# A gated network kernel's start: batch 1's k turned on TensorE, weights in longer runs, first loads issued by ScalarE, a new order of steps

## The chip, the cores and the metric

The kernel runs on one core of a Trainium2 chip. Its time is the device time of one execution in microseconds (us), taken as the median of three runs. The profile shows one further execution, instruction by instruction; its span is the time from its first instruction to the end of its last one.

## What is computed

For each of 8 batches, linear attention over 8 heads (576 rows, 64 channels a head) makes x, and a gated network works on x:

```python
q_s = softmax(q, axis=-1);  k_s = softmax(k, axis=2)        # k over its 576 rows
x = einsum('bhsd,bhde->bhse', q_s, einsum('bhsd,bhse->bhde', k_s, v))   # -> (8, 576, 512)
h = gelu_tanh(x @ w_in)                                      # w_in 512 x 1024
u, v = h[..., :512], h[..., 512:]
v_n = (v - mean(v)) / sqrt(var(v) + 1e-6) * g_ln
v_s = einsum('ts,bsd->btd', w_sg, v_n) + b_sg[None, :, None] # w_sg 576 x 576
out = x + (u * v_s) @ w_out                                  # w_out 512 x 512
```

w_in and w_out are float64; all other inputs and the output are float32.

## The kernel before

**Steps and order.** The program is a list of named steps, `PLAN`; each names a small function with a batch and the piece it works on. A step issues a few instructions on one engine, and every engine runs its own in the order of the list (line 163 for the engines, line 253 for TensorE), so the list is the queue of each engine and of SP, which issues all transfers. An instruction that waits holds up everything behind it on its engine. At the end of a step's name, `V`, `A` and `G` choose VectorE, ScalarE or GpSimd for it.

**Precision.** Every float32 operand of the large products is split into a high part that TensorE takes in its fast format and a low part; a product is high x high, high x low and low x high in one accumulation. w_in and w_out are float64, so each arrives as two 32-bit words and is made into float32 on the chip, then split: `wi_a` (ScalarE scales), `wi_b`, `wi_c`, `wi_d` (VectorE shifts and merges), `wi_h` (ScalarE writes the high part) and `wi_l` (the low part), once for each of w_in's eight pieces of 128 columns (512 KB), with `wo_*` for w_out's four; `ws_h` and `ws_l` split w_sg's five pieces. Pieces 0 to 3 of w_in make u, 4 to 7 make v.

**A batch.** `load_q`, `load_k`, `load_v` bring the inputs, each batch in two halves of four heads (the second number of a step). q: maximum, subtraction, exponential, sum, inverse, product, then a transpose to `qt`. Batch 0's q lies flat and is worked in two groups a half (`qf_*`, the third number) and turned by TensorE (`qtr_mm`, `qf_copy`); the other batches' q is turned by VectorE (`q_turn`). k: batch 0 arrives with its rows along the free axis (`k_turn`), so a maximum over rows is one instruction (`kr_max`), ScalarE takes the exponential (`kr_exp`), TensorE turns it back with ten transposes a half (`ktr_mm`) and ScalarE copies it out (`kr_copy`, `kr_rest`). Batch 1's k arrives the other way round: VectorE folds the rows (`k_ma`, `k_mb`, `k_mc`), TensorE turns the 128 partial maxima (`kt_mm`), VectorE reduces (`k_top`), TensorE spreads the result (`kb_mm`), VectorE subtracts (`k_sub`) and ScalarE takes the exponential (`k_exp`). Batches 2 to 7 use a fold on VectorE instead of TensorE. `kv_mm` forms k's product with v, `kv_scale` divides, and `xf_mm` (batch 0, in four pieces), `x_mm` (batch 1) or `xm_mm` make x; `xf_high`, `xf_low` and their like write its two parts.

**The network.** `hu_mm` makes a piece of u (batch 0 in two column groups, `hu_part`, emptied by `hu_gpart` with the gelu), `hv_mm` a row block of v, `hv_gelu`, `hv_sq`, `hv_stat`, `hv_pow`, `hv_norm`, `hv_high`, `hv_low` its normalisation, `sg_mm` the product with w_sg, `gate`, `gate_high`, `gate_low` the gating, `out_mm` the last product, `out_base`, `out_add`, `out_store` the end. TensorE writes large groups into three double PSUM banks in turn and small ones into two single banks in turn (`bank`), so a group waits until the one three (or two) before it is emptied. `warm` multiplies the identity by itself and its result is not read.

**Names that are shared.** The tile `x_l` has two buffers: batch 0's turned k lies in the first until `ktr_mm` has read it. The tile of q of one half is shared by all batches, so `load_q 1 1` waits until batch 0's second half was turned. `load_v 2 1` waits for `kv_mm 1 1`, which reads the tile it writes.

## Time and profile before

| | us |
|---|---|
| median of three runs (lowest, highest) | 498.81 (498.34, 499.73) |
| the profiled execution, its own time | 498.2 |
| its span | 496.4 |
| TensorE busy with matmuls | 483.7 (97%) |
| VectorE, ScalarE, GpSimd busy | 357.8, 285.8, 180.0 |
| transfers | 47.08 MB on SP's queue |

The granted TensorE clock is 0.999 of full over the span. Busy times are unions of an engine's instructions; matmuls overlap one another, so a busy TensorE may still be waiting in part. Most instructions stand under line 164, the helper that issues them, and all matmuls under line 253; they are told apart by their tiles (`ps<-x_h,wi_h` is a matmul of x's high part with w_in's). `x_lk` is the turned k, `raw_i_*` are w_in's words, `kk` is k, `km` its maxima, `qq` is q.

### The profile page before, as it was taken

The page shows a single profiled execution, that of the slowest core. Times are in us where ns is not written, and L with a number is a line of the kernel's source. Part 1 is how long each engine was busy: PE and PEld are TensorE (multiplying, and loading weights), DVE is VectorE, ACT ScalarE, POOL GpSimd, SP SyncE. Part 2 cuts the span into 40 slices and gives each one's busy share as a digit, 9 for nine tenths or more (in the row PEclk, how much of TensorE's full clock was granted, in tenths as well). Part 3 has the DMA queues.
Part 4 walks back from the last instruction along what each step waited for, and adds up shares of the span by engine and source line. Part 5 has one row for each costly group of instructions (what it writes and reads, how often), then busy time and mean ns, then how long its engine had stood idle before and what let it go on. Part 6 is the DMA issues. An engine that isn't in the chain of part 4 may idle for free.

```text
span 496.4 us, 9521 instructions
## 1 busy us (share of the span) xinstructions
PE 483.7 (97%) x3859; PEld 445.4 (90%) x3859; DVE 357.8 (72%) x608; ACT 285.8 (58%) x603; POOL 180.0 (36%) x138
## 2 busy tenths in 40 slices
...
GB/s 278 362 380 208 153 172 1 157 105 136 1 58 242 53 45 49 76 56 120 97 57 141 93 61 47 1 71 167 39 2 1 144 73 1 1 0 49 1 1 143
DMA packets 20911, 47.68 MB, mean 96 GB/s; under 512 B 1922, under 2 KB 9476, under 8 KB 20868
## 3 DMA queue, kind: packets, MB, share of 16 engines
q1 hardware_dynamic: 20868, 47.08, 27.7%
...
## 4 chain that ended last, share of the span: by engine, by line
PE 68%; DVE 18%; DMA 4%; ACT 4%; issue 3%; POOL 2%; SPq 1%; DVEq 0%; ACTq 0%; POOLq 0%
PE ps L253 68%; DVE km L164 3%; DMA raw_i_vnl<-w_in 2%; DVE qm L164 2%; DVE v L164 1%; DVE ot_i L164 1%; DVE qd L164 1%; DMA x_lk<-k_turn 1%; DVE kf L164 1%; POOL qq L164 1%; DVE ot_o L164 1%; DMA vv<-v 1%; DVE o L164 1%; SPq L164 1%; DVE vnl L164 1%
## 5 line engine op out<-in xcount | busy, mean ns | idle before, releaser
L164 POOL TENSOR_TENSOR rs<-ve,half 128x1 f32<-128x1 f32 (+1 forms) x37 | 30.4, 826 | 98.6 <-DVE ve L164 98.6
L253 PE MATMUL ps<-ws_h,vnl 128*128 128x288 f32 x256 | 55.0, 296 | 0.7 <-DVE vnl L164 0.7
L253 PE MATMUL ps<-ulow,wo_h 128*128 128x288 f32 x256 | 55.6, 296 | 0.0
L253 PE MATMUL ps<-gh,wo_h 128*128 128x288 f32 x256 | 55.5, 295 | 0.0
L253 PE MATMUL ps<-gh,wo_l 128*128 128x288 f32 x256 | 55.3, 295 | 0.0
L253 PE MATMUL ps<-ws_h,vnh 128*128 128x288 f32 x256 | 55.2, 297 | 0.0
L253 PE MATMUL ps<-ws_l,vnh 128*128 128x288 f32 x256 | 54.9, 296 | 0.0
L164 POOL TENSOR_TENSOR ulow<-u,gh 128x576 fp32r<-128x576 f32 x17 | 28.0, 1644 | 67.3 <-ACT gh L164 56.6
L164 POOL TENSOR_TENSOR qq<-qq,qm 128x1152 f32<-128x1152 f32 (+2 forms) x13 | 26.5, 2039 | 63.5 <-DVE qm L164 43.8
L164 DVE TENSOR_TENSOR u<-ps,u 128x576 f32<-128x576 f32 x32 | 23.9, 749 | 32.3 <-PE ps L253 32.2
L164 ACT ACT_TABLE_LOAD x34 | 43.6, 1283 | 5.8 <-PE ps L253 2.7
L164 ACT CAST gh<-u 128x576 fp32r<-128x576 f32 x32 | 21.1, 668 | 42.8 <-DVE u L164 42.7
L253 PEld LDWEIGHTS ps<-ws_h,vnh 128*128 128x128 f32 x256 | 41.5, 188 | 0.8
L253 PEld LDWEIGHTS ps<-ws_h,vnl 128*128 128x128 f32 x256 | 41.1, 188 | 0.9 <-DVE vnl L164 0.9
L253 PEld LDWEIGHTS ps<-gh,wo_h 128*128 128x128 f32 x256 | 41.3, 188 | 0.6
L253 PE MATMUL ps<-x_h,wi_h 128*128 128x288 f32 (+2 forms) x256 | 40.7, 299 | 0.7 <-ACT x_l L164 0.7
L253 PEld LDWEIGHTS ps<-gh,wo_l 128*128 128x128 f32 x256 | 41.3, 188 | 0.0
L253 PEld LDWEIGHTS ps<-ulow,wo_h 128*128 128x128 f32 x256 | 41.1, 188 | 0.1
L253 PE MATMUL ps<-wi_h,x_h 128*128 128x512 f32 (+1 forms) x148 | 41.0, 398 | 0.0
L253 PEld LDWEIGHTS ps<-ws_l,vnh 128*128 128x128 f32 x256 | 41.0, 188 | 0.0
L253 PE MATMUL ps<-wi_h,x_l 128*128 128x512 f32 (+1 forms) x148 | 40.9, 396 | 0.1
L253 PE MATMUL ps<-wi_l,x_h 128*128 128x512 f32 (+1 forms) x148 | 40.5, 395 | 0.0
...
## 6 DMA issues: line engine op xcount, KB each, us to landing
...
```

The source lines that it names most:

```text
L164: ins = op(*args, **kw)
L253: tc.keep_in_program_order(nc.tensor.matmul(*args, **kw))
```

## The change

Four things are changed together. Batch 1's k arrives turned as batch 0's does and goes through `kr_max`, `kr_exp`, `ktr_mm`, `kr_copy` and `kr_rest`; it lies in the second `x_l` buffer. w_in and w_out are laid out in memory by pieces, so that a partition's part of one piece is one run of 4096 bytes instead of four of 1024. The identity, the two bias rows and the two turned loads of batch 0's second half are issued by ScalarE, ahead of everything else on it. And the order of the steps and the engine of many of them (`V`, `A`, `G`) are new from the first step to the last; seven warm steps stand where eight did, three of them ahead of the first turned q instead of seven in a row. In the diff, `PLAN` is cut after the first `sg_mm` of either version.

```diff
 FOLD = [2, 3, 4, 5, 6, 7]
 ALONE = [0, 1]
-TURN = [0]
+TURN = [0, 1]
 FLAT = [0]
-SHAPES = [(B - len(FLAT), 2, P, 2, 18, 32), (len(FLAT), 2, P, 18, D), (B - len(TURN), 2, P, 5, 256), (len(TURN), 2, P, 2, S), (B, 2, P, 5, 4, D + 1), (DM, 2048), (1, DV), (5, P, WT), (1, WT), (DV, 1024), (P, P), (B, DM, S)]
+SHAPES = [(B - len(FLAT), 2, P, 2, 18, 32), (len(FLAT), 2, P, 18, D), (B - len(TURN), 2, P, 5, 256), (len(TURN), 2, P, 2, S), (B, 2, P, 5, 4, D + 1), (8, P, 1024), (1, DV), (5, P, WT), (1, WT), (4, P, 1024), (P, P), (B, DM, S)]
 
...
 PLAN = """
-kr_zero 0 1, load_q 0 1 1, qf_max 0 1 1, qf_sub 0 1 1 V, qf_exp 0 1 1, load_q 0 1 0, kr_zero 0 0, qf_max 0 1 0, qf_sub 0 1 0 G, qf_exp 0 1 0, load_eye
-warm 0, warm 1, warm 9, warm 7, warm 4, load_q 0 0 0, qf_max 0 0 0, warm 8, warm 6, qf_sum 0 1 1, load_k 0 0 1, kr_max 0 0 1, kr_exp 0 0 1
-load_q 0 0 1, qf_sub 0 0 0 G, qf_exp 0 0 0, qf_inv 0 1 1, qf_mul 0 1 1 G, qf_max 0 0 1, qf_sub 0 0 1 G, load_k 0 0 0, kr_max 0 0 0, kr_exp 0 0 0
-load_k 0 1 0, kr_max 0 1 0, kr_exp 0 1 0, load_w_in 1, qf_exp 0 0 1, wi_a 1, qf_sum 0 0 0, qf_inv 0 0 0, load_w_in 0, ktr_mm 0 0, qf_sum 0 1 0
-kr_copy 0 0, qf_sum 0 0 1, qf_inv 0 0 1, wi_a 0, wi_b 1, kr_rest 0 0, neg, load_k 0 1 1, kr_max 0 1 1, qtr_mm 0 1 1, load_v 0 0, qf_mul 0 0 0 G
-qtr_mm 0 0 0, wi_b 0, qf_mul 0 0 1 G, warm 2, qf_copy 0 1 1, qf_inv 0 1 0, qf_mul 0 1 0 G, kr_exp 0 1 1, qf_copy 0 0 0, load_w_in 2, wi_a 2, kv_mm 0 0
-qtr_mm 0 0 1, wi_c 0, kv_inv 0 0, load_w_in 3, kv_scale 0 0, wi_c 1, wi_d 0, qf_copy 0 0 1, wi_a 3, load_v 0 1, ktr_mm 0 1, kr_copy 0 1, qtr_mm 0 1 0
-qf_copy 0 1 0, wi_b 2, xf_mm 0 0 0, kr_rest 0 1, kv_mm 0 1, wi_b 3, xf_high 0 0 0, wi_c 2, wi_h 0, wi_c 3, wi_d 1, wi_h 1, wi_d 3, wi_h 3, load_w_sg 1
-wi_l 0 V, xf_low 0 0 0, xf_mm 0 0 1, wi_x 3, xf_high 0 0 1, kv_inv 0 1, kv_scale 0 1, xf_mm 0 1 0, xf_mm 0 1 1, wi_d 2, load_w_in 7, wi_a 7, wi_b 7
-xf_high 0 1 0, xf_neg 0 0 1, load_k 1 0, wi_c 7, k_ma 1 0, xf_high 0 1 1, xf_neg 0 1 0, wi_d 7, k_mb 1 0, xf_low 0 1 1, xf_low 0 0 1 A, hu_part 0 0 1
-load_w_in 4, wi_l 1 G, xf_low 0 1 0 A, load_q 1 1, k_mc 1 0, kt_mm 1 0, load_k 1 1, wi_a 4, wi_b 4, wi_h 2, hu_part 0 0 0, wi_l 2 G, hu_gpart 0 0 1
-hu_part 0 2 0, load_w_in 5, q_max 1 1, k_ma 1 1, k_mb 1 1, wi_c 4, wi_d 4, wi_h 7, k_mc 1 1, q_swapm 1 1, q_top 1 1, q_sub 1 1 G, hu_gpart 0 0 0
-wi_a 5, wi_b 5, wi_l 3 A, load_q 1 0, q_max 1 0, wi_h 4, hu_part 0 1 0, hu_gpart 0 2 0, hu_gpart 0 1 0, load_w_in 6, wi_a 6, kt_mm 1 1, k_top 1 1
-ws_h 1, hu_part 0 3 0, hu_gpart 0 3 0, q_swapm 1 0, k_top 1 0, kb_mm 1 0, load_w_sg 2, wi_b 6, wi_l 7 V, q_exp 1 1, load_w_out 3, wi_c 5, wi_c 6
-load_w_out 0, load_g, q_top 1 0, load_b, q_sub 1 0 G, wi_d 6, wi_h 6, k_sub 1 0 V, k_exp 1 0, hu_part 0 2 1, wi_d 5, wi_l 6 G, load_v 1 0, q_exp 1 0
-hu_part 0 1 1, wi_h 5, b_h, kb_mm 1 1, k_sub 1 1 V, k_exp 1 1, q_sum 1 0, load_w_sg 0, hu_part 0 3 1, q_swapd 1 0, q_sum 1 1, wi_l 4 G, kv_mm 1 0
-kv_inv 1 0, kv_scale 1 0, q_inv 1 0, q_swapd 1 1, wi_l 5 G, b_l G, q_inv 1 1, hv_mm 0 0, hv_gelu 0 0 A, load_w_out 2, hu_gpart 0 3 1, q_mul 1 0 0 V
-q_mul 1 0 1 G, q_turn 1 1, q_mul 1 1 1 G, q_turn 1 0, hu_gpart 0 1 1, load_w_sg 3, hv_mm 0 3, hv_gelu 0 3 A, load_v 1 1, hu_gpart 0 2 1, ws_h 2
-q_turn 1 3, kv_mm 1 1, x_mm 1 0, kv_inv 1 1, kv_scale 1 1, q_mul 1 1 0 G, q_turn 1 2, wo_a 3, wo_z 3, x_high 1 0, x_low 1 0, wo_a 0, wo_b 0, wo_c 0
-hv_mm 0 1, ws_h 0, wo_b 3 A, wo_d 3, load_w_out 1, wo_a 1, wo_a 2, hv_sq 0 0, hv_stat 0 0 A, hv_norm 0 0, hv_gelu 0 1 A, hv_sq 0 1, wo_b 2, ws_l 0 V
-wo_d 0, x_high 1 1, load_q 2 1, hv_stat 0 1 A, hv_sq 0 3, wo_b 1, wo_c 1, wo_d 1, x_mm 1 1, x_high 1 3, hv_mm 0 4, hv_pow 0 0, x_high 1 2
-hv_stat 0 3 A, hv_norm 0 3, x_neg 1 1, hv_mm 0 2, hv_pow 0 3, x_low 1 1 A, hv_gelu 0 4 A, wo_c 2, wo_d 2, hv_pow 0 1, ws_l 2 G, x_low 1 2, x_low 1 3
-load_w_sg 4, hv_high 0 0, hv_low 0 0, ws_h 4, hv_high 0 3, hv_low 0 3, hv_norm 0 1, load_k 2 1, hv_mm 1 3, hv_gelu 0 2, hv_sq 0 4, hv_stat 0 2
-hv_norm 0 2, hv_gelu 1 3 A, hv_mm 1 0, hv_mm 1 2, hv_high 0 1, hv_low 0 1, wo_h 2, hv_sq 1 3, ws_l 1 V, hv_gelu 1 0 A, k_ma 2 1, k_mb 2 1, hv_pow 0 2
-hv_high 0 2, hv_stat 0 4 A, hv_norm 0 4, hv_pow 0 4, tail_high 0, tail_again 0, ws_l 4 G, hv_stat 1 3 A, ws_h 3, k_mc 2 1, hv_mm 1 1, hv_pow 1 3
-k_fold 2 1, k_rota 2 1, hv_sq 1 0, load_q 2 0, wo_h 3, load_k 2 0, q_max 2 0, q_swapm 2 0, hv_low 0 2, ws_l 3 V, tail_low 0, sg_mm 0 3, hv_gelu 1 2
...
+load_eye A, load_b A, load_k 0 1 1 A, load_k 0 1 0 A, load_q 0 1 0, load_q 0 0 1, qf_max 0 1 0, qf_sub 0 1 0 G, qf_exp 0 1 0, qf_max 0 0 1
+kr_max 0 1 1, kr_exp 0 1 1, b_h, qf_sum 0 1 0, qf_inv 0 1 0, qf_sub 0 0 1 G, qf_mul 0 1 0 G, warm 11, load_q 0 0 0, qf_max 0 0 0, warm 9, warm 3
+qf_sub 0 0 0 G, kr_max 0 1 0, load_q 0 1 1, qf_max 0 1 1, qf_exp 0 0 1, qtr_mm 0 1 0, qf_sum 0 0 1, warm 2, kr_exp 0 1 0, ktr_mm 0 1, kr_zero 0 0
+qf_exp 0 0 0, qf_sum 0 0 0, qf_copy 0 1 0, load_w_in 3, wi_a 3, qf_inv 0 0 1, qf_inv 0 0 0, wi_b 3, qf_sub 0 1 1 G, qf_exp 0 1 1, load_k 0 0 1
+kr_max 0 0 1, qf_sum 0 1 1, kr_copy 0 1, load_w_in 2, wi_a 2, kr_exp 0 0 1, load_k 0 0 0, kr_max 0 0 0, kr_exp 0 0 0, qf_inv 0 1 1, qf_mul 0 0 0 G
+qf_mul 0 0 1 G, qf_mul 0 1 1 G, warm 8, load_k 1 1 0, kr_max 1 1 0, load_k 1 1 1, warm 10, qtr_mm 0 0 0, qf_copy 0 0 0, kr_rest 0 1, kr_exp 1 1 0
+warm 0, kr_max 1 1 1, kr_exp 1 1 1, wi_c 3, wi_b 2, qtr_mm 0 0 1, load_w_in 0, wi_a 0, ktr_mm 0 0, kr_rest 0 0, kr_copy 0 0, neg, load_v 0 1, wi_d 3
+qf_copy 0 0 1, load_w_in 1, wi_a 1, wi_c 2, kr_zero 0 1, kv_mm 0 1, wi_b 0, wi_d 2, wi_c 0, kv_inv 0 1, kv_scale 0 1, wi_d 0, wi_b 1, wi_c 1
+qtr_mm 0 1 1, qf_copy 0 1 1, ktr_mm 1 1, wi_h 2, wi_l 2 V, kr_zero 1 1, wi_h 3, load_v 0 0, kv_mm 0 0, kv_inv 0 0, wi_h 0, wi_d 1, kr_copy 1 1
+kv_scale 0 0, xf_mm 0 1 0, xf_high 0 1 0, xf_mm 0 1 1, xf_high 0 1 1, kr_zero 1 0, load_k 1 0 1, kr_max 1 0 1, xf_mm 0 0 0, xf_high 0 0 0, wi_h 1
+xf_low 0 1 0, load_w_in 5, xf_mm 0 0 1, xf_high 0 0 1, xf_low 0 1 1, wi_l 0 G, load_w_in 4, load_k 1 0 0, wi_l 3 G, xf_low 0 0 0, kr_exp 1 0 1
+kr_max 1 0 0, kr_exp 1 0 0, wi_l 1 G, hu_part 0 3 0, hu_gpart 0 3 0, wi_a 4, load_q 1 1, kr_rest 1 1, xf_low 0 0 1, hu_part 0 0 1, hu_part 0 2 0
+q_max 1 1, load_q 1 0, q_max 1 0, wi_b 4, q_swapm 1 0, wi_a 5 G, load_w_in 6, wi_a 6, load_w_in 7, hu_gpart 0 2 0, hu_gpart 0 0 1, wi_b 5
+hu_part 0 1 1, q_swapm 1 1, wi_c 4, wi_d 4, q_top 1 0, load_v 1 0, b_l G, wi_c 5, q_sub 1 0 V, wi_a 7, ktr_mm 1 0, kr_copy 1 0, q_top 1 1, kr_rest 1 0
+hu_gpart 0 1 1, load_w_out 2, q_exp 1 0, wi_h 4, wi_b 7, wi_c 7, wi_b 6, wi_c 6, wi_d 5, wi_h 5, wi_d 7, wi_d 6, wi_h 6, hu_part 0 3 1, wi_h 7
+q_sub 1 1 V, kv_mm 1 0, load_v 1 1, kv_mm 1 1, kv_inv 1 1, kv_inv 1 0, kv_scale 1 0, q_sum 1 0, kv_scale 1 1, q_exp 1 1, load_w_sg 1, wi_l 6 V
+wi_l 7 V, wi_l 4 G, q_swapd 1 0, q_inv 1 0, hu_part 0 1 0, hu_gpart 0 1 0, load_g, q_sum 1 1, q_mul 1 0 0 V, hu_part 0 2 1, wo_a 2, wo_b 2, wi_l 5 G
+hv_mm 0 0, q_swapd 1 1, hv_gelu 0 0 A, q_mul 1 0 1 G, load_v 2 1, q_inv 1 1, q_mul 1 1 1 G, hv_sq 0 0, wo_c 2, hu_gpart 0 2 1, hu_gpart 0 3 1
+load_w_out 0, wo_a 0, load_w_out 3, hv_mm 0 1, q_turn 1 0, hv_gelu 0 1 A, hv_sq 0 1, load_w_sg 0, hv_mm 0 3, hv_gelu 0 3 A, q_turn 1 1, x_mm 1 0
+x_high 1 0, hv_mm 0 2, wo_a 3, hv_stat 0 0 A, q_turn 1 3, hv_norm 0 0, wo_b 0, wo_c 0, load_w_sg 3, wo_d 2, wo_d 0, load_w_out 1, load_k 2 1, wo_a 1
+q_mul 1 1 0 G, q_turn 1 2, x_high 1 1, load_v 2 0, ws_h 0, hv_pow 0 0, hv_stat 0 1 A, hv_norm 0 1, x_low 1 0, load_w_sg 2, ws_h 2, x_mm 1 1
+x_high 1 2, x_low 1 1, x_high 1 3, load_q 2 0, wo_b 3, wo_c 3, load_q 2 1, wo_d 3, hv_gelu 0 2 A, wo_z 1, wo_b 1 A, wo_d 1, hv_pow 0 1, hv_sq 0 3
+hv_stat 0 3 A, hv_pow 0 3, hv_norm 0 3, hu_part 0 0 0, hv_high 0 0, hv_low 0 0, x_low 1 2, x_low 1 3, ws_l 0 G, hv_high 0 1, k_ma 2 1, k_mb 2 1
+k_mc 2 1, hv_low 0 1, q_max 2 0, wo_h 3, hv_mm 0 4, hv_gelu 0 4 A, ws_h 3, hv_sq 0 2, hv_sq 0 4, hv_stat 0 2 A, hv_pow 0 2, hv_norm 0 2, ws_l 2 G
+hv_high 0 3, hv_mm 1 3, hv_gelu 1 3 A, hv_low 0 3, q_swapm 2 0, hv_mm 1 0, hv_gelu 1 0, load_w_sg 4, hv_mm 1 2, ws_h 4, hv_mm 1 1, ws_h 1
+hv_stat 0 4 A, k_fold 2 1, hv_norm 0 4, q_max 2 1, hv_high 0 2, hv_pow 0 4, load_k 2 0, k_ma 2 0, k_mb 2 0, wo_h 0, tail_high 0, hv_sq 1 3, tail_low 0
+k_rota 2 1, k_maxa 2 1, hv_low 0 2, q_swapm 2 1, ws_l 4 V, ws_l 3 V, hv_gelu 1 2, tail_again 0, q_top 2 0, ws_l 1 G, k_mc 2 0, k_fold 2 0, sg_mm 0 0
...
@@ -253,8 +253,7 @@
         tc.keep_in_program_order(nc.tensor.matmul(*args, **kw))
 
 
-    w_in3 = w_in.rearrange("(c p) (n t) -> p c n t", p=P, t=2)
-    w_out3 = w_out.rearrange("(c p) (n t) -> p c n t", p=P, t=2)
+    w_in5, w_out5 = (w.rearrange("f p (c n t) -> f p c n t", c=4, t=2) for w in (w_in, w_out))
 
     def piece(kind, f):
         return slice(0, 4), slice(f * P, f * P + P)
@@ -342,12 +341,12 @@
         return scale, zero, shift, sign, rest, high, low_
 
     def load_w_in(f):
-        Y.dma_start(out=raw["i", f], in_=w_in3[:, piece("i", f)[0], piece("i", f)[1]])
+        Y.dma_start(out=raw["i", f], in_=w_in5[f])
 
     def load_w_out(f):
         if ("o", f) not in raw:
             raw_words("o", f // 2)
-        Y.dma_start(out=raw["o", f], in_=w_out3[:, piece("o", f)[0], piece("o", f)[1]])
+        Y.dma_start(out=raw["o", f], in_=w_out5[f])
 
     wi_a, wi_z, wi_b, wi_c, wi_d, wi_h_, wi_l_ = converter("i")
     wo_a, wo_z, wo_b, wo_c, wo_d, wo_h_, wo_l_ = converter("o")
@@ -387,9 +386,9 @@
 
     bias = [(v_s("b", j, at=j)[TL:TL + 1, 0:WT // 2], slice(j * (WT // 2), (j + 1) * (WT // 2))) for j in range(2)]
 
-    def load_b():
+    def load_b(E=Y):
         for r, cs in bias:
-            Y.dma_start(out=r, in_=b_sg[:, cs])
+            E.dma_start(out=r, in_=b_sg[:, cs])
 
     def b_h():
         for r, cs in bias:
@@ -402,8 +401,8 @@
     def load_g():
         Y.dma_start(out=g_bc, in_=g_ln.broadcast_to([P, DV]))
 
-    def load_eye():
-        Y.dma_start(out=eye, in_=identity)
+    def load_eye(E=Y):
+        E.dma_start(out=eye, in_=identity)
 
     def warm(n):
 
@@ -424,17 +423,14 @@
     def flat_q(b, h):
         return qq_s(b, h, at=h, shape=[P, 18, D])
 
-    def load_k(b, h, a=None):
+    def load_k(b, h, a=None, E=Y):
         if b not in TURN:
             Y.dma_start(out=kk_s(b, h, at=h), in_=k[b - sum(t < b for t in TURN), h])
         else:
-            Y.dma_start(out=turned(b, h, a), in_=k_turn[TURN.index(b), h, :, a])
-
-    def early(h):
-        return x_l("k", 0, at=0, shape=[P, 2, 2, S], dt=F32)[:, h]
+            E.dma_start(out=turned(b, h, a), in_=k_turn[TURN.index(b), h, :, a])
 
     def turned(b, h, a):
-        return u_s("k", b, h, a, at=2 * h + a) if b else early(h)[:, a]
+        return x_l("k", b, at=b, shape=[P, 2, 2, S], dt=F32)[:, h, a]
 
     def kr_zero(b, h):
         G.memset(kk_s(b, h, at=h)[TL:P, ST], 0.0)
@@ -934,6 +930,11 @@
     chan = np.arange(DM).reshape(2, 2, 2, D).transpose(0, 2, 1, 3).reshape(DM)
     order = [np.arange(S), np.r_[ST * P:S, 0:ST * P]]
     arr = {}
+
+    def pieces(w):
+        z = w.reshape(4, P, -1, P).transpose(2, 1, 0, 3)
+        return np.ascontiguousarray(z).reshape(-1, P, 512).view(np.int64)
+
     qo = np.stack([q[b][:, order[second(b)]] for b in range(B)])
     qs = qo[[b for b in range(B) if b not in FLAT]].reshape(-1, 2, 2, 2, 18, 32, 2, 32)
     arr["q"] = np.ascontiguousarray(qs.transpose(0, 1, 3, 6, 5, 2, 4, 7)).reshape(-1, 2, P, 2, 18, 32)
@@ -950,13 +951,13 @@
     vs[:, :S, :, :, :D] = v.transpose(0, 2, 1, 3).reshape(B, S, 2, 4, D)
     vs[:, :S, :, :, D] = 1
     arr["v"] = np.ascontiguousarray(vs.reshape(B, 5, P, 2, 4, D + 1).transpose(0, 3, 2, 1, 4, 5))
-    arr["w_in"] = np.ascontiguousarray(moe_w_in[chan]).view(np.int64)
+    arr["w_in"] = pieces(moe_w_in[chan])
     arr["g_ln"] = np.ascontiguousarray(moe_g_ln.reshape(1, DV))
     ws = moe_w_sg.T
     ws = np.concatenate([ws[:, ST * P:], ws], axis=1)
     arr["w_sg"] = np.ascontiguousarray(np.concatenate([ws, ws[ST * P:]], axis=0).reshape(5, P, WT))
     arr["b_sg"] = np.ascontiguousarray(np.concatenate([moe_b_sg[ST * P:], moe_b_sg]).reshape(1, WT))
-    arr["w_out"] = np.ascontiguousarray(moe_w_out[:, chan]).view(np.int64)
+    arr["w_out"] = pieces(moe_w_out[:, chan])
     arr["identity"] = np.eye(P, dtype=np.float32)
 
     nc = bacc.Bacc("TRN2", target_bir_lowering=False, num_devices=1, dynamic_dma_scratch_size=1024)

```

## Rows read from the trace of the kernel before

**Rows 1.** The page's busy times: busy us, share of the span, instructions.

```profile
PE 483.7 (97%) x3859; PEld 445.4 (90%) x3859; DVE 357.8 (72%) x608; ACT 285.8 (58%) x603; POOL 180.0 (36%) x138
```

**Rows 2.** Stretches of the span: from and to, length, then busy us and instructions of PE, PEld, DVE, ACT and POOL, the granted clock, the busy share of the DMA engines and GB/s.

```profile
2.00:4.00 2.00, 0.00 (x0) 0.00 (x0) 0.24 (x1) 0.00 (x0) 1.85 (x6) 1.00 0.93 310
4.00:6.00 2.00, 1.38 (x6) 1.38 (x7) 1.97 (x3) 0.53 (x1) 0.22 (x1) 1.00 0.85 189
10.00:11.00 1.00, 0.82 (x5) 0.63 (x4) 1.00 (x3) 0.63 (x3) 1.00 (x2) 1.00 1.10 377
24.00:26.00 2.00, 1.88 (x21) 1.10 (x20) 1.97 (x5) 1.68 (x3) 0.17 (x1) 1.00 1.07 406
10.90:26.80 15.90, 12.94 (x161) 9.20 (x161) 15.10 (x36) 15.09 (x29) 6.35 (x6) 1.00 1.07 371
26.90:42.40 15.50, 15.34 (x144) 14.85 (x144) 15.43 (x26) 15.26 (x30) 8.48 (x5) 1.00 1.05 363
42.40:72.90 30.50, 30.04 (x186) 21.91 (x183) 29.37 (x56) 27.42 (x66) 17.54 (x16) 1.00 0.45 159
100.00:150.00 50.00, 49.31 (x408) 44.48 (x407) 46.12 (x72) 33.12 (x72) 29.37 (x19) 1.00 0.24 80
```

**Rows 3.** The timeline of TensorE: start, us from the first to the end of the last of the group, instruction, tiles, size, how many, and in brackets what it waited for.

```profile
4.62 6.20 PE L253 MATMUL ps<-eye 128*128 128x128 f32 x28 [4.62 <-DMA eye<-identity]
...
11.78 1.31 PE L253 MATMUL ps<-eye,x_lk 128*128 128x128 f32 x10 [0.95 <-ACT x_lk L164]
...
26.88 0.85 PE L253 MATMUL ps<-x_h,wi_h 128*128 128x320 f32 x4 [0.68 <-ACT x_l L164]
...
42.41 1.20 PE L253 MATMUL ps<-wi_h,x_h 128*128 128x512 f32 x4
...
72.91 0.43 PE L253 MATMUL ps<-ws_h,vnh 128*128 128x288 f32 x2
73.18 0.43 PE L253 MATMUL ps<-ws_h,vnl 128*128 128x288 f32 x2
```

**Rows 4.** The chain that ended last, its pieces in order of time: start, us, what.

```profile
3.51 5.99 DMA x_lk<-k_turn
9.51 9.33 DMA raw_i_vnl<-w_in
```

**Rows 5.** Instructions grouped by tiles and shape, up to 130 us (TensorE's up to 70): how many, busy us, mean ns of one, idle time before them and its end.

```profile
L164 DVE TENSOR_REDUCE qm<-qq 128x36 f32<-128x1152 f32 x6 | 8.0, 1340 | 0.0
L164 DVE TENSOR_TENSOR km<-kk 128x512 f32<-128x512 f32 x6 | 4.1, 688 | 0.0
L164 DVE TENSOR_TENSOR kk<-kk,ps 128x1280 f32<-128x1280 f32 x2 | 3.0, 1480 | 0.0
L164 DVE TENSOR_REDUCE km<-x_lk 128x1 f32<-128x576 f32 x4 | 2.9, 742 | 0.0
L164 DVE TENSOR_TENSOR km<-km,kk 128x256 f32<-128x256 f32 x6 | 2.5, 416 | 0.0
L164 DVE TENSOR_TENSOR wi_l<-ot_i,wi_h 128x512 fp32r<-128x512 f32 x2 | 1.4, 680 | 0.0
L164 DVE TENSOR_TENSOR qq<-qq,qm 128x1152 f32<-128x1152 f32 x1 | 1.4, 1357 | 0.0
L164 DVE TENSOR_REDUCE kt<-ps 128x2 f32<-128x256 f32 x2 | 0.7, 414 | 0.0
L164 ACT ACTIVATE kk<-kk 128x1280 f32<-128x1280 f32 x4 | 5.1, 1274 | 1.6 <-POOL kk L164 1.3 <-DVE kk L164 0.3
L164 ACT ACTIVATE x_lk<-x_lk,km 128x576 f32<-128x576 f32 x4 | 3.0, 774 | 1.8 <-DVE km L164 1.8
L164 ACT COPY kk<-ps 128x1024 f32<-128x1024 f32 x2 | 2.0, 992 | 0.0
L164 ACT COPY kk<-ps 64x256 f32<-64x256 f32 x2 | 0.7, 361 | 0.0
L164 POOL TENSOR_TENSOR qq<-qq,qm 128x1152 f32<-128x1152 f32 x5 | 11.7, 2332 | 18.1 <-DVE qm L164 13.7 <-issue 4.3
L253 PE MATMUL ps<-eye,kt 128*128 128x128 f32 x4 | 0.8, 285 | 0.2 <-DVE kt L164 0.2
L253 PE MATMUL ps<-eye,km 128*128 128x128 f32 x4 | 0.8, 278 | 0.0
```

**Rows 6.** The timeline of SP's queue at the start, columns as in the third group.

```profile
0.72 0.85 SPq L164 DMA_DIRECT2D qq<-q_flat  x2
1.62 0.42 SPq L164 DMA_DIRECT2D eye<-identity  x1
```

**Rows 7.** The timeline of VectorE and ScalarE where the text names a start or an end, columns as in the third group.

```profile
0.72 1.28 ACT L164 ACT_TABLE_LOAD   x1 [0.72 <-PEq L962]
3.76 0.82 DVE L164 TENSOR_REDUCE qm<-qq 128x10 f32<-128x640 f32 x1 [3.76 <-DMA qq<-q_flat]
5.47 0.74 ACT L164 ACTIVATE qq<-qq 128x640 f32<-128x640 f32 x1 [3.47 <-DVE qq L164]
7.18 0.69 DVE L164 TENSOR_REDUCE qm<-qq 128x8 f32<-128x512 f32 x1 [1.14 <-DMA qq<-q_flat]
25.00 1.23 ACT L164 CAST x_h<-ps 128x512 fp32r<-128x512 f32 x2 [0.31 <-PE ps L253]
27.34 0.82 DVE L164 TENSOR_TENSOR x_l<-ps,x_h 128x640 fp32r<-128x640 f32 x1
73.01 0.82 DVE L164 TENSOR_TENSOR ws_l<-ghws,ws_h 128x640 fp32r<-128x640 f32 x1
```

161 lines of the change are left out of this document (80 added, 81 removed).

## The prediction

> **What bounds the kernel now.** I read the page's busy times first. TensorE is busy 97% of the span [rows 1], so the question is where the other 3% lies and whether the busy time is all needed. The stretches answer it: from 26.9 us on TensorE misses 0.16 us up to 42.4 and 0.46 us up to 72.9, and between 100 and 150 us another 0.69 [rows 2]. The slack is ahead of that. In the timeline of TensorE [rows 3] the reader sees that it multiplies the identity by itself from 4.62 to 10.8 us, turns the first k at 11.78, and begins the first useful dense group (`hu_part`) only at 26.88; `hv_mm` follows at 42.41 and the first `sg_mm` at 72.91. Before 26.9 VectorE and ScalarE each work 15.1 of 15.9 us and the transfers run at 371 GB/s [rows 2]; the chain of what ended last goes through the fourth load of batch 0's k, then through a load of w_in that lands at 18.86, then through VectorE [rows 4]. So three things share the start (transfers, ScalarE, VectorE), and VectorE stays near full far beyond it (29.37 of 30.5 us up to 72.9). From there the time is TensorE's work, which the new order keeps.
>
> **The change part by part.**
>
> *Batch 1's k.* On VectorE each head loses `k_ma` 0.69, `k_mb` 0.42, `k_mc` 0.42, `k_top` 0.41 and `k_sub` 1.48, 3.42 us, and gains two maxima at 0.74 [rows 5]: for two heads 6.84 - 2.97 = 3.9 us less. ScalarE loses two exponentials of 1.27 and gains four of 0.77, two copies of 0.99 and two of 0.36, 5.80 - 2.55 = 3.3 us more [rows 5]. GpSimd clears two tails, hidden: it works 6.35 of 15.9 us [rows 2]. TensorE loses the four small transposing groups, 0.8 + 0.8 us [rows 5], and gains two groups of ten transposes at 1.31 [rows 3], one of them ahead of `hu_part`, where TensorE has 3 us free (12.94 of 15.9) [rows 2]. Of the work after 26.88 it thus has 1.6 - 1.3 = 0.3 us less. The turned k sits in the second `x_l` buffer, which nobody needs before `x_low 1`.
>
> *Runs of 4096 bytes.* A stretch of w_in alone moved 377 GB/s, one of k and q in long runs 406 [rows 2], 7%. The first four w_in loads, 2.1 MB, are then 0.4 us shorter (2.1/377 against 2.1/406), nothing if the difference is chance. In the new order only `wi_a 3` stands close to its load; I count it inside the start.
>
> *ScalarE's issues.* The identity, two bias rows and two loads of k are five issues at about 0.42 us [rows 6], 2.1 us. ScalarE has nothing before its first exponential, for which it waits 3.5 us (it begins at 5.47) [rows 7], so they are hidden; behind them stand only its table load and that exponential. The table load (0.72 to 2.0) [rows 7] may stand ahead of them: the identity is then issued at 2.0 instead of 0.72, against 1.62 before [rows 6]. It took 3.0 us from issue to its first use (1.62 to 4.62) [rows 3, 6], so it is there by 5.0 at the latest, ahead of the first turned q. SP is spared the same 2.1 us. What that can give shows in the transfers: 310 GB/s from 2 to 4 us, but 189 from 4 to 6, when SP was still issuing [rows 2]. Filling that lull with the rate of its neighbour is (310 - 189) x 2 = 0.24 MB, or 0.7 us at 371 GB/s. In the other direction, the two queues share the rate: q's second piece (320 KB, VectorE's second instruction) now competes with k.
> [...]
>
> *The new order, up to `hu_part`.* `hu_part 0 3 0` needs `xf_high 0 0 0` of ScalarE and, a microsecond later, `xf_low 0 0 0` of VectorE. VectorE has 39 steps up to there against 41 up to the like one before (`xf_low 0 1 1`, ended at 28.16) [rows 7]: four subtractions or conversions of 512 or 640 columns, a shift and two maxima of kk go, three maxima at 0.74 and two subtractions at 0.68 come, 0.8 us less. ScalarE has 31 against 29 (up to `xf_high 0 1 1`, ended at 26.23) [rows 7]: two exponentials 1.55, a copy 0.99 and the two bias copies (0.7, an estimate from the 0.36 of the copy of 64 rows) come, a scaling and an `xf_high` go, about 0.62 each by the 1.23 of two [rows 7]: 2.0 us more. That gives 28.2 if ScalarE waits as before; following both queues by hand with loads landing 0.7 us sooner I get 26.6. I take 27.6, +0.7 on 26.88, with the ends -0.3 and +1.3.
>
> *Up to `sg_mm`.* `ktr_mm 1 0` takes the PSUM bank that `hu_gpart 0 0 1` must empty, and this stands on ScalarE behind a table load, `wi_a 4`, `kr_rest 1 1`, `q_swapm 1 0` (which waits for `q_max`), and `wi_a 6`; by its queue about 1.3 us after TensorE is ready (0 to 1.9). Behind that instruction all of TensorE waits. Less the 0.6 us that TensorE missed here before (0.16 + 0.46), +0.7. Beside it VectorE: up to `ws_l 3` it loses 3.9 (k) and gains 2 x 1.36 for `q_sub`, which leaves GpSimd (2.33 there), and by the other moves (more `xf_low`, `wi_l` and `x_low` at about 0.7, and batch 2's `q_max` at 1.34 pulled ahead, less `hv_stat`, `qf_sub` and two `ws_l`) some 3.8: 2.6 us more [rows 5]. Before, `ws_l 3` ended at 73.83 and `sg_mm` needs it about 22 matmuls in, 2.9 us after 72.91 (two in 0.27) [rows 3]: 2.0 us to spare. So VectorE alone would hold `sg_mm` back by 0.6, less than the path through TensorE: 0.7 - 0.3 + 0.7 = 1.1. If VectorE's start slips too, its path is the longer one.
>
> *After it.* TensorE's work is the same. I let the new order win half of the 0.69 us lost around 100 to 150: -0.4. In the end the last matmul, addition and store are the same.
>
> *Sum.* 1.1 - 0.4 = +0.7 on the profiled execution, 496.4 + 1.8 = 498.2, gives 498.9. The median of the runs is 498.81, 0.6 above that execution, so I forecast 499.5. A difference under 0.3%, 1.5 us, can't be told from none here.
>
> **The rivals.** *No measurable change (0.40)* is the forecast: its own range is 497.3 to 500.3.
>
> *Faster: the start closes up (0.27).* The lull from 4 to 6 us is filled (-0.7) and w_in is shorter (-0.4), so `hu_part` begins at 25.8; 0.3 less work, no new wait and the 0.6 gone, 0.7 later: -2.7, 496.1. For it speaks that the chain goes through loads up to 18.86 [rows 4]; against it ScalarE's 2.0 us more. It decides once `xf_high 0 0 0` ends before 25.5.
>
> *Slower: VectorE starves at the start and carries the lag (0.18).* It began at 3.76 and waited once, 1.14 us [rows 7]. If `qf_max 0 0 1` waits for q until about 5.8 behind k's two loads, 1.5 us are lost on the queue that has 2.6 us more to do up to `ws_l 3`: 2.6 + 1.5 - 2.0 = +2.1, and about 0.5, an estimate, for three `gate_low` now on GpSimd, which took 2.33 for `q_sub` where VectorE takes 1.36: 501.4. It decides once VectorE's lag on `ws_l 3` passes the 2.0 us.
>
> *Slower: the clock rises late (0.15).* [...]
> [...]
>
> That the edit of the runs does nothing is inside the first case.
>
> **How the numbers follow.** Faster by over 0.3% 0.27, within 0.40, slower 0.33. The range reaches to the middle of the faster case (496.1) and past that of the first slower one, 502.4; about 1 in 10 is left on each side.
>
> **What would show it.** Right: `hu_part` first at 27 to 28 us, a TensorE wait of about 1 us at the second turn of batch 1's k, first `sg_mm` at 73.5 to 74.5, the stretch behind it as dense as before. Wrong: warm matmuls or transposes still 0.21 us apart after 15 us (clock); VectorE idle over 2 us before 8 us (starved); `hu_part` before 26; or new waits of TensorE after 75 us, for which I have no term.

## The result and the profile after

The changed kernel takes 503.05 us (median of 5 runs, 501.52 to 503.61) where the kernel before, run beside it, takes 498.81: a ratio of 1.0080, 95% interval 1.0067 to 1.0093. Measured again later it took 502.92 against 498.94, 1.0087 (1.0070 to 1.0104). I had forecast 499.5 in a range up to 502.4: it is slower by some 4 us, and past the range.

The profiled execution has a span of 501.3 us against 496.4, so 4.9 us are to be found. First the page's busy times, which answer [rows 1], then the stretches that answer [rows 2], all in the same columns (the second fence has all engines).

```profile
PE 482.6 (96%) x3858; PEld 445.4 (89%) x3858; DVE 350.4 (70%) x608; ACT 287.3 (57%) x612; POOL 161.4 (32%) x135
```

```profile
2.00:4.00 2.00, 0.00 (x0) 0.00 (x0) 0.07 (x1) 0.00 (x0) 1.50 (x4) 1.00 0.95 308
4.00:6.00 2.00, 1.88 (x9) 1.88 (x10) 1.43 (x2) 1.46 (x2) 1.25 (x2) 1.00 0.94 272
6.00:8.00 2.00, 1.05 (x5) 0.76 (x4) 0.00 (x0) 0.46 (x1) 1.01 (x1) 1.00 0.99 351
10.90:28.40 17.50, 15.20 (x177) 12.48 (x177) 16.83 (x38) 16.81 (x32) 9.96 (x13) 1.00 1.03 386
28.40:44.00 15.60, 15.35 (x174) 14.83 (x175) 15.39 (x27) 15.30 (x29) 7.10 (x7) 1.00 0.64 211
44.00:73.40 29.40, 29.39 (x154) 22.17 (x153) 28.87 (x51) 27.01 (x68) 16.17 (x13) 1.00 0.56 204
100.00:150.00 50.00, 46.07 (x390) 41.33 (x389) 42.30 (x72) 25.24 (x60) 17.15 (x13) 1.00 0.27 89
```

TensorE has no more work than before, VectorE and GpSimd have less; time was lost in waits. The timeline of TensorE, which answers [rows 3], dates them.

```profile
4.12 2.93 PE L253 MATMUL ps<-eye 128*128 128x128 f32 x12 [4.12 <-DMA eye<-identity]
11.06 1.12 PE L253 MATMUL ps<-eye,qq 128*128 128x128 f32 x4 [4.01 <-POOL qq L164]
...
12.82 2.34 PE L253 MATMUL ps<-eye,x_lk 128*128 128x128 f32 x10
14.96 1.34 PE L253 MATMUL ps<-eye 128*128 128x128 f32 x8
...
28.38 0.72 PE L253 MATMUL ps<-x_h,wi_h 128*128 128x256 f32 x4
...
35.23 1.31 PE L253 MATMUL ps<-eye,x_lk 128*128 128x128 f32 x10 [0.25 <-ACT u L164]
...
44.01 1.10 PE L253 MATMUL ps<-wi_h,x_h 128*128 128x512 f32 x4
...
73.41 0.43 PE L253 MATMUL ps<-ws_h,vnh 128*128 128x288 f32 x2
...
126.19 0.73 PE L253 MATMUL ps<-wi_h,x_l 128*128 128x512 f32 x2 [1.76 <-DVE x_l L164]
...
133.05 0.80 PE L253 MATMUL ps<-ws,vn 128*128 128x288 f32 x4 [1.99 <-DVE vn L164]
...
495.88 0.40 PE L253 MATMUL ps<-gh,wo_h 128*128 128x288 f32 x1 [0.55 <-DVE o L164]
```

`hu_part` begins 1.5 us later (28.38 against 26.88), but the first `sg_mm` only 0.5 (73.41 against 72.91): between them 1.0 is won, because TensorE now misses 0.25 + 0.01 there instead of 0.16 + 0.46 and is busy 0.6 less (15.35 + 29.39 against 15.34 + 30.04). Behind `sg_mm` TensorE misses 3.93 us from 100 to 150 instead of 0.69, +3.2: nearly all of it in two waits, for `x_l` (1.76) and `vn` (1.99). At the end a wait of 0.55 is new, and from the last matmul to the end of the span it is 0.3 more. That is 0.5 + 3.2 + 0.55 + 0.3 = 4.6 of the 4.9; small stalls of either sign make up the rest.

Three causes are to be read from the rows.

**The start.** Timeline of ScalarE's queue and of VectorE:

```profile
0.72 0.42 ACTq L164 DMA_DIRECT2D eye<-identity  x1
1.16 0.79 ACTq L164 DMA_DIRECT2D vb<-b_sg  x2
1.98 2.30 ACTq L164 DMA_DIRECT2D x_lk<-k_turn  x2
8.03 0.75 DVE L164 TENSOR_REDUCE km<-x_lk 128x1 f32<-128x576 f32 x1 [2.42 <-DMA x_lk<-k_turn]
```

VectorE stands 2.42 us for the first k, issued at 1.98 and landed at 8.0. All four pieces of q had been issued by SP before 2.6. By 8.0 the transfers had moved (308 + 272 + 351) x 2 = 1.86 MB, about all that was issued in the first four microseconds (q 1.18, k 0.59, the identity 0.07, from the shapes): k came in with the last of q, whose third and fourth piece took 5.5 and 6.5 us from issue to landing.

**The wait for `x_l`.** Timelines of SP's queue and VectorE:

```profile
109.23 0.36 SPq L164 DMA_DIRECT2D out<-o  x1
109.69 1.89 SPq L164 DMA_DIRECT2D kk<-k  x1
116.11 0.69 DVE L164 TENSOR_TENSOR km<-kk 128x512 f32<-128x512 f32 x1 [2.43 <-DMA kk<-k]
124.92 1.21 DVE L164 TENSOR_TENSOR x_l<-ps,x_h 128x1024 fp32r<-128x1024 f32 x1
```

`load_k 3 0` (the second row, `kk<-k`) stands in SP's queue behind `out_store 0 0`, which waits for its addition until 109.2. The load lands at 116.1; VectorE stands for it, and `xm_low 2 1` (124.92), further back in its queue, is what TensorE then waits for.

**The wait for `vn`.** Timelines of VectorE and GpSimd, and the group of that addition (min/median/max in ns):

```profile
128.27 3.87 DVE L164 TENSOR_TENSOR o<-x_h,x_l 128x576 f32<-128x576 f32 x1
132.25 0.74 DVE L164 SCALAR_TENSOR_TENSOR vn<-v,rs,vn 64x512 fp32r<-64x512 f32 x1
128.73 2.80 POOL L164 TENSOR_TENSOR o<-x_h,x_l 128x576 f32<-128x576 f32 x2
L164 DVE TENSOR_TENSOR o<-x_h,x_l x11: 715/750/3872, 102.0 to 488.1; 128x576 f32<-128x576 f32 x11
```

`out_base 1 3` on VectorE takes 3.87 us where its like takes 0.75. It ends 0.6 us after GpSimd's two additions (131.53), and `tail_low 1` (132.25) stands behind it.

### The profile page after: what moved, and what is told of

Its sections match the earlier page's. It is cut to its first block, busy times and chain, and to the rows that moved or that the text cites. A ratio compares the mean times of both kernels' runs of the same rounds, so it can differ in the third digit from the quotient of the medians.

```text
span 501.3 us, 9526 instructions
## 1 busy us (share of the span) xinstructions
PE 482.6 (96%) x3858; PEld 445.4 (89%) x3858; DVE 350.4 (70%) x608; ACT 287.3 (57%) x612; POOL 161.4 (32%) x135
## 4 chain that ended last, share of the span: by engine, by line
PE 79%; DVE 10%; ACT 5%; DMA 4%; issue 1%; ACTq 0%; POOL 0%; SPq 0%; POOLq 0%; DVEq 0%
PE ps L253 79%; DMA kk<-k 3%; DVE km L164 2%; DVE o L164 2%; DMA x_lk<-k_turn 1%; DVE vnl L164 1%; DVE qd L164 1%; DVE v L164 1%; ACT x_lk L164 1%; DVE qq L164 1%; DVE x_l L164 1%; ACT kk L164 1%; ACT x_h L164 1%; DVE qm L164 1%; ACT L164 1%
## 5 line engine op out<-in xcount | busy, mean ns | idle before, releaser
L164 POOL TENSOR_TENSOR rs<-ve,half 128x1 f32<-128x1 f32 (+1 forms) x37 | 29.0, 788 | 116.8 <-DVE ve L164 116.8
L164 POOL TENSOR_TENSOR ulow<-u,gh 128x576 fp32r<-128x576 f32 x17 | 25.2, 1483 | 58.5 <-ACT gh L164 52.8
L253 PE MATMUL ps<-x_h,wi_l 128*128 128x288 f32 (+2 forms) x256 | 39.9, 296 | 0.0
```

Source lines behind the costliest of these rows:

```text
L164: ins = op(*args, **kw)
L253: tc.keep_in_program_order(nc.tensor.matmul(*args, **kw))
```

## The experiments

All are timed beside the kernel before. In the table the first `hu_part`, the first `sg_mm` and what TensorE missed from 100 to 150 us are of the profiled execution (26.88, 72.91 and 0.69 in the kernel before). x_after is the changed kernel once more. The diffs of `PLAN` are shortened to the steps around a move, without its line breaks.

| kernel | median us | before | ratio (95%) | hu_part | sg_mm | missed 100-150 |
|---|---|---|---|---|---|---|
| after | 503.05 | 498.81 | 1.0080 (1.0067-1.0093) | 28.38 | 73.41 | 3.93 |
| x_after | 502.92 | 498.94 | 1.0087 (1.0070-1.0104) | 28.93 | 73.95 | 3.28 |
| e1_port | 500.75 | 499.08 | 1.0030 (1.0016-1.0043) | 27.87 | 72.87 | 1.73 |
| e2_k3 | 500.85 | 499.08 | 1.0042 (1.0024-1.0059) | 29.02 | 74.08 | 1.81 |
| e3_both | 499.67 | 499.08 | 1.0001 (0.9986-1.0017) | 27.93 | 72.99 | 0.87 |
| e4_qfirst | 502.40 | 499.08 | 1.0057 (1.0034-1.0080) | 27.42 | 72.42 | 3.25 |
| g4_kfirst | 500.36 | 498.73 | 1.0041 (1.0025-1.0057) | 26.47 | 71.48 | 3.21 |
| g5_warm | 500.97 | 498.73 | 1.0046 (1.0030-1.0062) | 28.27 | 73.11 | 1.98 |
| g3_sync2 | 501.42 | 498.94 | 1.0048 (1.0033-1.0063) | 26.64 | 71.64 | 2.91 |
| g1_runs | 497.84 | 498.73 | 0.9980 (0.9970-0.9990) | 25.62 | 71.65 | 0.70 |
| g2_turn | 510.06 | 498.73 | 1.0228 (1.0212-1.0243) | 26.95 | 84.38 | 0.69 |
| g2b_turn | 510.78 | 498.94 | 1.0248 (1.0225-1.0270) | 28.08 | 85.06 | 0.69 |
| h1_best | 497.32 | 498.94 | 0.9971 (0.9960-0.9982) | 26.35 | 71.41 | 0.10 |

The five kernels whose start is that of the changed one (after, x_after, e1, e2, e3) begin `hu_part` between 27.87 and 29.02: one start differs from another by half a microsecond to either side, and smaller differences say nothing.

**The two late waits.** e1 moves GpSimd's two additions, e2 the load, e3 both.

```diff
-k_maxa 3 0, out_base 1 1 G, tail_low 1, hu_gelu 1 1, sg_mm 1 0, q_exp 3 1, load_q 3 0, out_base 1 0 G, k_maxb 3 1, k_sub 3 1 G, gate 1 0, gate_high 1 0, gate_low 1 0 G
+k_maxa 3 0, tail_low 1, hu_gelu 1 1, sg_mm 1 0, q_exp 3 1, load_q 3 0, k_maxb 3 1, k_sub 3 1 G, gate 1 0, gate_high 1 0, gate_low 1 0 G, out_base 1 1 G, out_base 1 0 G
```

> The changed kernel with two additions of GpSimd (out_base 1 1 and 1 0) moved behind its gate_low 1 0, so that they no longer run while VectorE does out_base 1 3. Theory: that VectorE addition took 3.87 us instead of 0.75 because GpSimd's two additions ran from 128.73 to 131.53 beside it and VectorE stood until they ended; with them away it takes 0.75, tail_low 1 ends before TensorE asks for it, TensorE's wait of 2.0 us for vn goes, and the kernel takes about 501.1 (503.05 less 2.0). Rival: the long addition is VectorE's own lateness (its wait for k before it), and the wait for vn stays at 1 to 2 us: 502.5 to 503.1.

```diff
-hu_gelu 1 3, load_v 3 1, out_base 0 1 G
+hu_gelu 1 3, load_v 3 1, load_k 3 0, out_base 0 1 G
...
-hv_pow 1 2, load_k 3 0, hu_mm 1 2
+hv_pow 1 2, hu_mm 1 2
```

> The changed kernel with one issue moved on SyncE: the load of batch 3's second k head stands behind the load of v 3 1 and not behind the first store of batch 0's output. Theory: the load waited at the head of the queue behind that store until 109.23, landed at 116.1, and VectorE stood 2.43 us for it; this made TensorE wait 1.8 us for x_l. Issued some 14 us earlier it lands before 105, VectorE's wait goes, the wait for x_l falls under 0.3, and the wait for vn keeps 1.4 to 2.0: 500.8 to 501.3. Rival: VectorE is late there from its own load, the wait for x_l stays over 1 us and the time is within 0.7 of 503.05.

> The two moves together. If the two waits of TensorE after 120 us are the whole of what the later stretch lost, both go: 503.05 less 1.8 and 2.0, 499.3, within 0.5. If something else is late right behind them (gate_low 1 0, k_sub 3 1 on GpSimd), a new wait of 1 us or more shows after 134 us and the time is 500.3 or more.

VectorE and GpSimd in e1, at the place where the addition took 3.87:

```profile
126.31 0.74 DVE L164 TENSOR_TENSOR o<-x_h,x_l 128x576 f32<-128x576 f32 x1
127.59 0.75 DVE L164 SCALAR_TENSOR_TENSOR vn<-v,rs,vn 64x512 fp32r<-64x512 f32 x1 [0.45 <-ACT vn L164]
133.44 2.82 POOL L164 TENSOR_TENSOR o<-x_h,x_l 128x576 f32<-128x576 f32 x2
```

The same instruction takes 0.74 when GpSimd's additions run elsewhere, `tail_low 1` now waits for ScalarE and not behind the addition, and TensorE's wait for `vn` is gone. The kernel is 2.3 us faster than the changed one, near what was expected, but in part by luck: the wait of 2.0 was exchanged for a new one of 1.02, and the wait for `x_l` was 1.27 shorter in the profiled execution. In e2 the load is issued at 98.03 and TensorE's wait for `x_l` is gone; the wait for `vn` stays (1.81), and the time is 500.85, as expected. In e3 both are gone and the kernel is as fast as the one before. So these two waits, with nothing else altered, carry about 3.4 us of the 4. What e3 missed of its 499.3 is the new wait further on, 0.87 there, and it is the same collision at another place. In e3 TensorE's timeline, then VectorE's, then GpSimd's:

```profile
143.06 1.20 PE L253 MATMUL ps<-wi_h,x_h 128*128 128x512 f32 x4 [0.87 <-DVE kvt L164]
136.69 1.23 DVE L164 TENSOR_TENSOR qm<-qm,qs 128x36 f32<-128x36 f32 x1
137.84 1.49 DVE L164 SCALAR_TENSOR_TENSOR qd<-qd,qe 128x36 f32<-128x36 f32 x1
134.92 2.94 POOL L164 TENSOR_TENSOR kk<-kk,km 128x1280 f32<-128x1280 f32 x1
137.83 1.45 POOL L164 TENSOR_TENSOR ulow<-u,gh 128x576 fp32r<-128x576 f32 x1
```

The additions, moved behind `gate_low 1 0`, push GpSimd's `k_sub 3 0` and `gate_low 1 1` beside two small steps of VectorE (`q_top 3 0`, `q_inv 3 1`). These end when GpSimd's end and take 1.23 and 1.49 us, where the changed kernel has 0.51 and 0.18; `kv_scale 3 0`, behind them in VectorE's queue, is what TensorE waits for.

The wait for `x_l` differs between executions of one order: 1.76 in after, 1.08 in x_after, 0.49 in e1, none in g5, as the load, issued between 108.6 and 110.3 in these four, lands 4.5 to 6.4 us later. So behind the store it has little or no time to spare, and what that costs is partly chance; e3 and e1, with the load early and late, differ by 0.3%.

**The start.** e4 changes VectorE's order, g4 ScalarE's issues, g3 puts these on SP, g5 keeps TensorE busy.

```diff
-kr_max 0 1 1, kr_exp 0 1 1, b_h, qf_sum 0 1 0, qf_inv 0 1 0, qf_sub 0 0 1 G
+qf_sum 0 1 0, qf_inv 0 1 0, kr_max 0 1 1, kr_exp 0 1 1, b_h, qf_sub 0 0 1 G
```

> The changed kernel with one step of VectorE moved at the start: the sums and reciprocals of q's first piece stand ahead of the first maximum of k, in the time in which VectorE waits for k (5.6 to 8.0 us). Theory: the first turned q waited 4.0 us (until 11.06) for work that stood behind k in VectorE's queue; now it comes at about 9, VectorE has 1.1 us of its work done before k lands, TensorE is busy earlier and is at the upper clock for k's first turn (ten transposes in 1.3 us instead of 2.34); the first hu_part comes at 27.0 to 27.6 instead of 28.38, and 1 us of the time goes: 502.0. Rival: the start is set by k's landing at 8.0 and by ScalarE's queue behind it; the first hu_part stays within 0.4 of 28.38 and the time within 0.4 of 503.05.

```diff
-load_eye A, load_b A, load_k 0 1 1 A, load_k 0 1 0 A, load_q 0 1 0, load_q 0 0 1
+load_k 0 1 1 A, load_eye A, load_k 0 1 0 A, load_b A, load_q 0 1 0, load_q 0 0 1
```

> The changed kernel with ScalarE's five issues in another order: the first load of k, the identity, the second load of k, the bias. The first k is then issued at 0.72 instead of 1.98 us. Theory: its landing at 8.0 us, for which VectorE stood 2.4 us, sets the start; it lands at 6.5 to 7.2, the first turned q comes about 1 us sooner and hu_part begins at 27.0 to 27.6 instead of 28.4: 502.1 (503.05 less 1). Rival: the loads share the 16 engines and what k gains q loses, or ScalarE's queue binds: hu_part within 0.4 of 28.4, 502.6 to 503.4.

```diff
-load_eye A, load_b A, load_k 0 1 1 A, load_k 0 1 0 A, load_q 0 1 0, load_q 0 0 1
+load_q 0 1 0, load_q 0 0 1, load_eye, load_k 0 1 1, load_k 0 1 0, load_b
```

> The changed kernel with its five issues taken from ScalarE and put on SyncE, behind q's first two pieces: identity, the two loads of k, the bias, then q's other two. Theory: the first k, issued at 1.98 by ScalarE behind the identity and the bias, is issued at about 2.1 by SyncE behind q and the identity, so it lands near 8.0 as before; hu_part within 0.5 of 28.4 and the time within 0.7 of the changed kernel. That would say that ScalarE's issues as ordered here won nothing. Rival: q's last two pieces, issued 2 us later, make VectorE wait and hu_part comes 1 us later: 504; or k gains because fewer queues share the engines: 502.

```diff
-warm 9, warm 3, qf_sub 0 0 0 G
+warm 9, warm 3, warm 21, warm 22, warm 23, warm 24, warm 25, warm 26, warm 27, warm 28, qf_sub 0 0 0 G
```

> The changed kernel with eight more warm steps after its third, so that TensorE works through the 4.0 us in which it waited for the first turned q. [...] Rival: the start is bound by VectorE's and ScalarE's queues and not by the turn; hu_part stays within 0.3 of 28.4 and the time at 502.7 to 503.3.

First g3: SP's queue and VectorE. Then g4: ScalarE's queue and VectorE (its first maximum of q, then of k). Then TensorE in g5.

```profile
2.10 0.91 SPq L164 DMA_DIRECT2D x_lk<-k_turn  x2
3.69 0.83 SPq L164 DMA_DIRECT2D qq<-q_flat  x2
6.30 0.75 DVE L164 TENSOR_REDUCE km<-x_lk 128x1 f32<-128x576 f32 x1 [1.17 <-DMA x_lk<-k_turn]
```

```profile
0.72 0.40 ACTq L164 DMA_DIRECT2D x_lk<-k_turn  x1
4.51 0.69 DVE L164 TENSOR_REDUCE qm<-qq 128x8 f32<-128x512 f32 x1 [4.51 <-DMA qq<-q_flat]
6.32 0.74 DVE L164 TENSOR_REDUCE km<-x_lk 128x1 f32<-128x576 f32 x1
```

```profile
4.06 7.15 PE L254 MATMUL ps<-eye 128*128 128x128 f32 x44 [4.06 <-DMA eye<-identity]
11.93 1.25 PE L254 MATMUL ps<-eye,x_lk 128*128 128x128 f32 x10
28.27 0.64 PE L254 MATMUL ps<-x_h,wi_h 128*128 128x256 f32 x4 [0.29 <-issue]
```

g3 contradicted me. Issued by SP at 2.10, no earlier than by ScalarE (1.98), k lands at 6.3 instead of 8.0, because q's third and fourth piece now follow it; `hu_part` comes at 26.64 and the kernel is 1.5 to 1.9 us faster. The time is near the second rival's 502, but its reason, fewer queues, is not the one: in g4 ScalarE issues as much as before, only k first, and VectorE begins on k at 6.32 without a wait; q came later instead (4.51, in after 3.93), and `hu_part` comes at 26.47. So it is not which engine issues; it is what else has been issued when k is. Nor is it the rate in g3, where the transfers move 319, 290 and 303 GB/s in the three stretches from 2 to 8 us, no more than in after; in g4 they move 278, 401 and 399, and no run separates what that adds. What the second queue cost in after: q's last two pieces, not needed before k, were in flight beside and ahead of it (all four pieces issued by 2.52; the first k, issued at 1.98, landed at 8.0).

e4 fills VectorE's wait with other work and wins 1 us at `hu_part` at most (27.42), as expected, but k's ten transposes took 2.40 us there, so not by a faster turn; its time, 502.40, can't be told from the changed kernel's (the intervals overlap). g5 settles that: with TensorE unbroken up to 11.2 us the ten transposes take 1.25 us, where after's take 2.34 behind the 4.01 us pause; yet `hu_part` comes at 28.27, within the spread of the unaltered start. g3 and g4 say the same: the ten transposes take 2.34 us in g3 and 1.25 in g4, and their `hu_part` are 0.17 apart. What the slower turn costs is no more than that spread: so TensorE did not set that start, and ScalarE and VectorE, each busy over 16.8 of its last 17.5 us, did. (g5 is faster by 2.1 us; in its profiled execution TensorE misses 1.95 less from 100 to 150, the absent wait for `x_l`.)

**One part alone.** g1 is the kernel before with only the weights in runs of 4096 bytes (its diff shows one line of several); g2 and g2b are the kernel before with only batch 1's k turned. g2's diff gathers the steps of one half, which stand apart in `PLAN`; the other half is changed alike, and g2b's text says what it moves.

```diff
-    w_in3 = w_in.rearrange("(c p) (n t) -> p c n t", p=P, t=2)
+    w_in5, w_out5 = (w.rearrange("f p (c n t) -> f p c n t", c=4, t=2) for w in (w_in, w_out))
```

> The kernel before, its order and its queues kept, with w_in and w_out alone in runs of 4096 bytes. Theory: the loads of w_in move 400 GB/s or more instead of 377, the four of the start are 0.4 us shorter, and no step waits on the last of them long enough to matter: 498.4 to 499.2, the same within 0.3%. Rival: shorter loads push k and q of batch 1 forward and the start closes up by 1 us: 497.8. If the new layout itself costs (4096-byte runs land later as a whole), it shows here: over 500.

```diff
-load_k 1 1, k_ma 1 1, k_mb 1 1, k_mc 1 1, kt_mm 1 1, k_top 1 1, kb_mm 1 1, k_sub 1 1 V, k_exp 1 1
+load_k 1 1 0, load_k 1 1 1, kr_max 1 1 0, kr_max 1 1 1, kr_zero 1 1, kr_exp 1 1 0, kr_exp 1 1 1, ktr_mm 1 1, kr_copy 1 1, kr_rest 1 1
```

> The kernel before, its order and its queues kept as far as they can be, with batch 1's k turned by TensorE alone: the maxima and exponentials stand where the two-stage maximum and the subtractions stood, the turning and the copies where kb_mm, k_sub and k_exp stood. Theory: VectorE loses 3.9 us before 73 us and ScalarE gains 3.3, TensorE loses 0.3: 498.2 to 499.2, the same. Rival: ScalarE, busy to 15.1 of 15.9 us before hu_part, carries its 3.3 us into the loop and TensorE waits for u or kk 1 to 3 us between 30 and 55: 500 to 502.

> The kernel before with batch 1's k turned by TensorE alone, now with the loads, maxima and exponentials of both heads ahead of the first gelu, and one gelu (hu_gpart 0 2 1) moved up. Theory: TensorE stood 8.6 us in the first try because the exponentials stood between gelus, two table loads of 1.28 more, and all of TensorE stood behind the turn; with them ahead of the first gelu that wait falls under 2 us and the time is 498.5 to 501. Rival: ScalarE's four exponentials (3.1 us) ahead of the first gelu hold back every u behind them, TensorE waits for u 2 to 3 us: 501 to 503.

g1 hits the first rival: 0.2% faster. The stretch from 10 to 11 us, 377 GB/s before [rows 2], moves 425; from 10.9 us to just before `hu_part` it is 394 against 371:

```profile
10.00:11.00 1.00, 0.32 (x3) 0.32 (x4) 1.00 (x2) 1.00 (x2) 1.00 (x1) 1.00 1.04 425
25.62 0.86 PE L253 MATMUL ps<-x_h,wi_h 128*128 128x320 f32 x4 [0.68 <-ACT x_l L164]
```

and `hu_part` comes 1.3 us sooner, most of which arrives at the end (0.9).

g2 and g2b miss everything expected of them, at 510 and 511 us. In g2 one half of a block of u (block 2's second) is overwritten in PSUM before it is read, so its time is that of the same instructions with other values. In g2b TensorE loses 7.7 of the 46.6 us from 28.4 to 75, the most in

```profile
50.16 1.43 PE L253 MATMUL ps<-x_h,wi_h 128*128 128x320 f32 x4 [4.40 <-ACT u L164]
```

a wait for a gelu on ScalarE, behind q's exponentials, k's copies and table loads (1.28 us each). The groups of four matmuls right behind it take 1.27 to 1.43 us where their like took 0.74 to 0.83 before the wait (the granted clock is 0.93 over the stretch from 28.4 to 75 us, 1.00 in the next one to 100), so more was lost there than the wait itself. What the turned k costs by itself can't be read from these two, since my placing of its steps is part of it; what they show is that the turned k, in an order that was not made for it, came 11 to 12 us dearer, and that the new order hides its work on ScalarE (0.25 us at `ktr_mm 1 0`, row 35.23 above).

**Together.** h1 has g4's issues and e2's load, the two additions further back, and the last block's half matmuls apart:

```diff
-out_mm 7 2, out_base 7 2 G, out_add 7 2, out_mm 7 1, out_store 7 2, out_mm 7 0, out_base 7 0 V, out_add 7 0, out_store 7 0, last_mm 7 0, last_add 7 0, last_store 7 0, out_base 7 1 G, out_add 7 1, out_store 7 1, last_mm 7 1
+out_mm 7 2, out_base 7 2 G, out_add 7 2, out_base 7 0 V, last_mm 7 0, last_add 7 0, last_store 7 0, out_mm 7 1, out_store 7 2, out_base 7 1 G, out_add 7 1, out_store 7 1, out_mm 7 0, out_add 7 0, out_store 7 0, last_mm 7 1
...
-out_base 1 1 G
-out_base 1 0 G
+out_base 1 2 G, out_base 1 1 G, out_base 1 0 G
```

> The changed kernel with four moves: k first among ScalarE's issues, the load of batch 3's second k head ahead of the store, GpSimd's two additions of batch 1 behind its out_base 1 2, and in the end the half matmuls of the last block apart (the first half ahead of out_mm 7 1), so that the second half does not wait for the addition of the first. Theory: the losses add up: 1.9 at the start, 1.8 and 2.0 in the waits for x_l and vn, no new wait for kvt, 0.6 at the end: 503.0 less 6.3 is 496.7, faster than the kernel before by 0.4%. Rival: with those gone VectorE is late somewhere else between 100 and 150, and the time is 498 to 499.5.

It takes 497.32, faster than both kernels (0.9971 of the one before, 0.9960 to 0.9982). The waits for `x_l` and `vn` before 150 and the one at the end are gone, and so is the one for `kvt`. Against the expected 496.7 it falls 0.6 us short, and TensorE has a wait for `x_l` at 156.6 that after does not have, later than the rival had placed it. In TensorE's and GpSimd's timelines:

```profile
156.64 1.20 PE L254 MATMUL ps<-wi_h,x_h 128*128 128x512 f32 x4 [1.35 <-DVE x_l L165]
147.63 4.62 POOL L165 TENSOR_TENSOR o<-x_h,x_l 128x576 f32<-128x576 f32 x3
152.21 1.00 POOL L165 TENSOR_TENSOR rs<-ve,half 128x1 f32<-128x1 f32 x1
```

The three additions in a row hold back GpSimd's own next step (`rs`, of `hv_pow 2 0`), for which ScalarE waits 4.43 us (2.30 in after) and behind which it makes batch 3's `x_h`, and VectorE `x_l`. That is read from the rows; no run moved the additions once more.

## Why the prediction was wrong, point by point

- **After `sg_mm`: the step that failed.** I wrote that TensorE's work is the same (right) and let the new order win 0.4 of the 0.69 lost around 100 to 150; it lost 3.2 more there, and 0.8 in the end, where I had put nothing. This term had no working: every other step was followed through its queue, this one was a guess in the direction of improvement, for a list that was new from the first line to the last. I did not ask what the 0.69 waited for; it was the same collision of VectorE with GpSimd that then cost 2 us (the rows are in the last section). Both causes stood in the lists: `load_k 3 0` behind `out_store 0 0` on SP, and VectorE's `out_base 1 3` beside GpSimd's `out_base 1 1` and `1 0`, with `tail_low 1` behind it. I named new waits after 75 us as what would make the prediction wrong, and gave them no chance and no price. Without the two waits (e3) the time is 499.67, close to the 499.5 that I forecast; that agreement is partly luck, by the next points.
- **The start, forecast +0.7 (ends -0.3 and +1.3), came out at +1.5.** I took ScalarE's issues as hidden and worth up to 0.7. In the order in which they stood they cost 1.7 to 1.9 (28.38 against 26.64 and 26.47 in g3 and g4). I saw that the two queues share the rate (308 GB/s together from 2 to 4 us, where one queue moved 310 [rows 2]), but looked at q, which VectorE needs second; it is k that shared and came late. The rival "VectorE starves" had the size right (1.5 us lost, idle over 2 us before 8 us) and the transfer wrong; its consequence, VectorE holding back `sg_mm`, did not come. Of the two numbers between which I chose 27.6, the 28.2 by ScalarE's added work is near 28.38 by chance, since g4 has the same work; the 26.6 from following the queues, with loads that come in time, is what g3 and g4 do.
- **Up to `sg_mm`, forecast +0.7 - 0.3, came out at -1.0.** The wait at `ktr_mm 1 0` was 0.25 and not 1.3, near the lower of my ends; the 0.6 of waits that had been there went. With 0.6 less busy time where I had 0.3, two errors cancelled in part: first `sg_mm` at +0.5, where I had +1.1.
- **The runs** gave 0.9 us alone where I had at most 0.4.
- **The clock, a chance of 0.15**, was an estimate of mine: no run shows a granted clock that rises late; it is 1.00 in every stretch of the start, before and after. What the runs show in its place is the time of the same instructions. In after the ten transposes took 2.34 us at 12.82, behind a wait of 4.01, and four transposes of q 1.12 at 11.06 but 0.60 at 16.14; ten took 1.31 in the kernel before, behind a wait of 0.95, and 1.25 in g5 without one. All that was ahead of `hu_part`, and what it cost, g5 puts within the spread of the start.
- **Faster by 2.7, "the start closes up"**, comes nearest to h1 (`hu_part` at 26.35 where I had 25.8, 497.32 where I had 496.1); in the change as it was, the order of the issues and the two late waits stood in its way.
